# Seven f64 weight chunks loaded during the attention, the first gather moved to ScalarE's queue, and the ranking of the experts put ahead of all narrowing

## Chip, cores and metric

The kernel runs on one core of one Trainium2 chip. The metric is the device time of one execution in microseconds (us). A core has a matrix engine (TensorE, PE in the profile; PEld is its weight load), VectorE (DVE), ScalarE (ACT), GpSimd (POOL) and SyncE (SP, which here only issues transfers), 16 transfer engines, an on-chip memory of 128 partitions and the psum banks into which TensorE writes. ScalarE and GpSimd have transfer queues of their own as well.

## What is computed

Three stages follow one another; the host does no arithmetic.

```
scores = where(mask, q @ k.T / 8, -1e9)       # q, k, v: 2 x 8 heads x 576 x 64; half the heads
x = softmax(scores) @ v                       # see 32 keys back, half every 32nd key
x = x.transpose to (1152 tokens, 512)
logits = x @ w_gate; expert = argmax          # 8 experts, at most 288 tokens each, in order
y = relu(x_e @ w1[e]) @ w2[e]                 # w1: 8 x 512 x 1024, w2: 8 x 1024 x 512, f32
x = softmax weight of the chosen expert * y
out = max(0.01 h, h) @ w_out, h = x @ w_in    # w_in: 512 x 2048, w_out: 2048 x 512, f64 (16 MB)
```

## The kernel before

**Attention** (some 0 to 85 us). Sixteen units of two heads and one half each go through the engines in an order written out by hand: LOOP has a line of letters for each of 14 iterations, TAIL (lines 40 to 45) the order of the rest. A letter stands for a step of one engine. L issues loads on SP's queue (lines 808 to 824): at iteration 8 the second batch's local q and k, at 10 its v rows. While units finish, route_idx (line 606) picks each token's expert and its place among that expert's tokens, in four groups of tokens; scatter (g0 to g11 in TAIL, line 671) writes 96 token rows each with an indirect transfer on GpSimd's queue into the DRAM buffer xs, sorted by expert. route_gate (line 314) computes the softmax weights of a group's tokens: one exponential on ScalarE and six short steps on VectorE. route_order (o in TAIL, line 257) then ranks the experts by their number of tokens: a matmul sums the counts, and 16 short steps on VectorE give the experts' order (`by[:, 0]`, line 274), the largest load (`most`, line 279) and the offsets (`by[:, 1]`, line 282).

**The branch.** Lines 968 and 977 load these numbers into registers: the order on SP and ScalarE, the offsets on VectorE, `most` on every engine. GpSimd clears the four yT buffers (line 976), which lie where the attention's buffers were. Line 981 is a branch that every engine takes part in: its body, not run here, treats experts with too many tokens. It uses the same psum banks and transfer counters as the code behind it, so each engine passes an event there.

**Experts** (100 to 246 us). start() (line 896) issues on SP's queue the gather of the first expert's rows from xs (x_rows, line 840), two pairs of weights (load_pair, line 112: 512 KB of w1 on line 119, as much of w2 on line 121), the second expert's gather and two pairs more. A block of four matmuls of the identity (line 913) is issued ahead of the first transposes (x_cols, lines 846 to 850), which turn the gathered rows. Each expert then has eight steps of layer 1 (line 856, relu on ScalarE, line 857) and eight of layer 2 (line 863), two steps behind; VectorE adds an expert's four banks into yT (line 872) and so frees them. Pairs have four buffers (NA). Each step of layer 1 ends with pump(1, NX), one step of narrowing.

**Narrowing.** VectorE and ScalarE turn the f64 weights of the last stage into two f32 halves each, high and low. There are 16 chunks of 1 MB, loaded as two parts (load_wide, line 132; the tag wide has NW = 4 buffers, so four parts come in the attention, at iteration 10). A part takes three bit steps on VectorE (top, line 152; sign, 157; low, 162; the last also loads the part NW further on), a cast on ScalarE (high, 167) and a subtraction on VectorE (rest, 171). Six steps make a chunk; pump(n, used) runs the next n while fewer than `used` chunks are done, and NX = 10 chunks are to be narrowed before the last stage, into the tag hlx of a pool that takes the attention's space. start() runs the remaining route_gate and pump(6, NX) ahead of the branch's successors.

Within a `manual_schedule` block each engine keeps the written order. Where the steps of one block fall among those of another is left to a scheduler: it drew the gate and the first narrowing of start() ahead of the branch, in turns with route_order.

**Last stage** (246 to 455 us). Three blocks of 384 tokens, TensorE bound; narrowing of the other six chunks goes on beside the first block.

Of the kernel before, what the change touches and what calls it, by code (L numbers as in the profile page):

```python
# [8 lines left out]
F32 = mybir.dt.float32  # L9
F32R = mybir.dt.float32r  # L10
# [29 lines left out]

TAIL = """
sw ay0 pw ay1 cv my Rk Lk ev r1 dv xv az0 az1 Rk fy cw ew Lv Lk Rj dw cy Rj mz0 xw Lv Rv ey Rv Rl Lw Rl mz1 fz0
fz1 sy Lw i2 dy i2 cz0 xy i2 Rw i2 i2 cz1 sz0 ez0 i2 ez1 Ly i2 dz0 i2 Rw dz1 xz Ly i2 sz1 Ly i2 g5 Ry Lz Lz Lz
i3 i2 i2 i3 g6 i3 Rz Ry i3 Rz g7 wz1 i3 i3 Wy wz0 i3 i3 g8 i3 i3 g9 i3 i3 o g10 g11
# [5 lines left out]
def kernel(ctx, tc, q, k, v, w_gate, w1, w2, w_in, w_out, out, cap):  # L50
# [26 lines left out]
    wts = ctx.enter_context(tc.tile_pool(name="wts", bufs=1))  # L77
    dram = ctx.enter_context(tc.tile_pool(name="dram", bufs=1, space=bass.MemoryType.DRAM))
# [19 lines left out]
    NA, NX = 4, 10  # L98
# [24 lines left out]

    def hl_tile(i):
        a, b = chunks[i].shape[1:]
        tag, nb = ("hlx", NX) if i < NX else ("hl", NA) if i < NX + NA else ("hly", len(chunks) - NX - NA)
        hls[i] = pools[tag].tile([128, 2, a, b], F32R, tag=tag, name=tag, bufs=nb)
# [14 lines left out]
    def narrow(j):  # L142
        i, h = j // 2, j % 2
        a, b = chunks[i].shape[1:]
        hs = slice(h * a // 2, (h + 1) * a // 2)
        got = {}

        def top():
            if h == 0:
                hl_tile(i)  # L150
            tmp = got["tmp"] = wts.tile([128, a // 2, b], U32, tag="tmp", name="tmp", bufs=3)
            nc.vector.tensor_scalar(out=tmp, in0=wides[j][:, :, :, 1], scalar1=3, scalar2=0x3FFFFFFF,
                                    op0=ALU.logical_shift_left, op1=ALU.bitwise_and)

        def sign():
            tmp = got["tmp"]
            nc.vector.scalar_tensor_tensor(out=tmp, in0=wides[j][:, :, :, 1], scalar=0xC0000000, in1=tmp,
                                           op0=ALU.bitwise_and, op1=ALU.bitwise_or)

        def low():  # L160
            tmp = got["tmp"]
            nc.vector.scalar_tensor_tensor(out=tmp, in0=wides.pop(j)[:, :, :, 0], scalar=29, in1=tmp,
                                           op0=ALU.logical_shift_right, op1=ALU.bitwise_or)
            load_wide(j + NW)

        def high():
            nc.scalar.copy(out=hls[i][:, 0, hs], in_=got["tmp"].bitcast(F32))  # L167

        def rest():
            hl = hls[i]  # L170
            nc.vector.tensor_tensor(out=hl[:, 1, hs], in0=got["tmp"].bitcast(F32), in1=hl[:, 0, hs].bitcast(F32),  # L171
                                    op=ALU.subtract)

        return [top, sign, lambda: (low(), high()), rest]

    narrows = []
    spent = [0]

    def pump(n, used):
        for _ in range(n):  # L180
            if spent[0] < len(narrows) and spent[0] // 6 < used:
                narrows[spent[0]]()
                spent[0] += 1
# [143 lines left out]
    last = {}  # L327
# [5 lines left out]
    with ExitStack() as actx:  # L333
# [271 lines left out]
        def route_idx(r):  # L605
# [7 lines left out]
            if r == 2:  # L613
                t = wts.tile([TT, 2, 2 * G, E], F32, tag="tmp", name="gates", bufs=3)
                last["dl"], last["kp"] = t[:, 0], t[:, 1]
            own = slice((r - 2) * G, (r - 1) * G)
            dl = last["dl"][:, own] if r > 1 else att.tile([TT, G, E], F32, tag="dl", name="dl", bufs=2)
# [24 lines left out]
            kp = last["kp"][:, own] if r > 1 else att.tile([TT, G, E], F32, tag="kp", name="kp", bufs=2)  # L642
# [39 lines left out]
        with tc.manual_schedule():  # L682
# [62 lines left out]
            for it in range(NU - 2):  # L745
                us = todo.get(it, [])
                cur, prev = units[it], units[it - 1] if it else None
                for op in LOOP[it].split():
# [18 lines left out]
                    elif op == "L":  # L767
# [13 lines left out]
                        if it == 10:  # L781
                            load_vl(1)
                            for j in range(NW):
                                load_wide(j)
# [16 lines left out]
            for op in TAIL.split():  # L801
                if op in gens:
                    run(gens[op], 1)
                elif op == "o":
                    route_order(bank_t(), att)
                elif op[0] == "g":
# [81 lines left out]
    with ExitStack() as ectx:  # L888
# [7 lines left out]
        def start():  # L896
            xrs[0] = x_rows(wts, 0, 0, 2, WR[0] // 2, nc.sync)
            load_pair()
            load_pair()
            xrs[1] = x_rows(wts, 1, 0, 2, WR[1] // 2, nc.sync)  # L900
            for _ in range(NA - 2):
                load_pair()
            late = []
            for j in range(2 * len(chunks)):
                p = narrow(j)
                narrows.extend([p[0], lambda s=p[1], f=late: (s(), [x() for x in f]), p[2]])
                late = p[3:]
            narrows.append(late[0])
            route_gate(last["dl"], last["kp"], slice(TB, 2 * TB), ep)
            pump(6, NX)  # L910
            warm = bank("S")
            for i in range(2):
                nc.tensor.matmul(warm.rearrange("p (a b) -> p a b", a=4), ident,
                                 ident.unsqueeze(1).to_broadcast([128, 4, 128]), start=(i == 0), stop=(i == 1))
            xe_new(0)
            for c in range(KD):
                x_cols(xrs[0], xes[0], c, 2, WR[0] // 2, "L")

# [12 lines left out]
        def step(lay, e, m):  # L931
            p = (e * NF + m) // 2
            if lay == 1:
# [7 lines left out]
                pump(1, NX)  # L941
# [24 lines left out]
        with tc.manual_schedule():  # L966
# [10 lines left out]
            over = nc.values_load(most, min_val=0, max_val=3 * NT)  # L977

# [47 lines left out]
    with ExitStack() as mctx:  # L1026
# [6 lines left out]
        for i in range(len(items) + LAG):  # L1033
            if i < len(items):
# [5 lines left out]
                while spent[0] < min(len(narrows), 6 * (m // 2 * 2 + 2) + 2) and ch == 0:  # L1040
                    pump(1, 999)
# [67 lines left out]
```

## Time and profile before

| | us |
|---|---|
| median of 3 runs | 462.95 |
| runs | 462.08 to 463.44 |
| profiled execution, its own time | 461.31 |
| its span in the trace | 459.6 |
| TensorE busy | 428.0 (93%) |
| VectorE busy | 209.2 (46%) |
| ScalarE busy | 159.0 (35%) |
| GpSimd busy | 71.4 (16%) |

The times are those of whole executions, the span is what the trace covers of one of them. A busy share is an average over stages with different limits, so stretches are read one by one. The clock that TensorE was granted has two levels, 1.0 (2.4 GHz) and 0.5 (1.2 GHz); the mean of a stretch can lie between. A wait names the engine, the line and what came last before the wait ended. An event or a branch of an engine's sequencer has a q behind the engine's name (DVEq).

### The profile page before, as it was taken

How to read it: one execution, taken by the hardware profiler on the slowest of the kernel's cores; microseconds unless marked ns; L12 is line 12 of the kernel's file. 1: busy time of each engine (PE TensorE's matmuls, PEld its weight loads, DVE VectorE, ACT ScalarE, POOL GpSimd, SP SyncE). 2: the span in 40 equal slices, each digit the busy share in tenths (PEclk: the TensorE clock that was granted, in tenths of full speed). 3: DMA queues.
4: the chain of work that ended last, by engine and by line, in shares of the span. 5: the costliest groups of instructions: out<-in, count | busy, mean ns of one | idle time of the engine just before them, and what ended most of it. 6: DMA issues, size and time to landing. Idle time of an engine off the chain costs nothing.

```text
span 459.6 us, 7850 instructions
## 1 busy us (share of the span) xinstructions
PE 428.0 (93%) x2980; PEld 398.6 (87%) x2980; DVE 209.2 (46%) x472; ACT 159.0 (35%) x379; POOL 71.4 (16%) x127
## 2 busy tenths in 40 slices
PE   5999999159999999988999999999999999999994
PEld 5899999039999999987899898899899989998993
DVE  4677878851253351542302687783222233222220
ACT  4768776112222222222122433442422233322222
POOL 6252542730000001560000000000200000200002
PEclk9999999659999999999999999999999999999998
DMA  7999640369999899999992044200100000100001
GB/s 170 194 323 177 187 154 19 106 196 319 352 330 313 299 302 310 332 249 306 352 352 66 8 133 135 91 3 0 71 0 1 0 0 1 68 1 0 1 0 69
DMA packets 56566, 68.84 MB, mean 150 GB/s; under 512 B 20137, under 2 KB 36521, under 8 KB 56521
## 3 DMA queue, kind: packets, MB, share of 16 engines
q1 hardware_dynamic: 53691, 61.74, 45.0%
q0 software_dynamic: 1872, 4.73, 3.0%
q10 hardware_dynamic: 958, 1.80, 1.4%
q8 instruction: 25, 0.41, 0.4%
q14 instruction: 20, 0.16, 0.1%
HBM read 60.38 MB, written 7.87 MB: 149 GB/s over the span
## 4 chain that ended last, share of the span: by engine, by line
issue 44%; PE 24%; DMA 6%; POOL 2%; POOLq 0%; ACT 0%; SPq 0%; ACTq 0%
PE psS L856 12%; PE psL L863 11%; DMA xr<-xs 2%; DMA pair<-in_moe_w_dram 2%; POOL out_dram L1078 2%; DMA tb<-tab 1%; PE psT L849 1%; PE psL L849 0%; POOLq L1105 0%; ACT ht L857 0%; POOL gap L663 0%; SPq L121 0%; SPq L119 0%; ACT xe L850 0%; POOLq L1078 0%
## 5 line engine op out<-in xcount | busy, mean ns | idle before, releaser
L856 PE MATMUL psS<-xe,pair 128*128 128x128 f32 (+6 forms) x512 | 79.6, 300 | 1.9 <-DMA pair<-in_moe_w_dram 1.9
L863 PE MATMUL psL<-ht,pair 128*128 128x128 f32 (+6 forms) x512 | 79.8, 300 | 0.0
L856 PEld LDWEIGHTS psS<-xe,pair 128*128 128x128 f32 x512 | 73.0, 193 | 2.4 <-issue 2.3
L863 PEld LDWEIGHTS psL<-ht,pair 128*128 128x128 f32 x512 | 70.7, 190 | 0.5
L1053 DVE TENSOR_TENSOR r<-psS,r 128x384 f32<-128x384 f32 x48 | 26.7, 557 | 82.6 <-ACT r L1052 82.6
L857 ACT ACTIVATE ht<-psS 128x128 f32<-128x128 f32 (+6 forms) x64 | 19.2, 300 | 109.4 <-PE psS L856 101.6
L1052 ACT ACTIVATE r<-psS 128x384 f32<-128x384 f32 x48 | 23.6, 492 | 86.8 <-PE psS L1050 86.7
L1078 POOL DMA_INDIRECT out_dram<-o,tb x9 | 8.7, 962 | 239.9 <-ACT o L1077 239.1
L1047 PE MATMUL psS<-yc,hlx 128*128 128x384 f32 x120 | 40.6, 338 | 0.9 <-ACT yc L884 0.9
L1048 PE MATMUL psS<-yc,hlx 128*128 128x384 f32 x120 | 40.7, 339 | 0.0
L1056 DVE TENSOR_TENSOR g<-r,g 128x384 fp32r<-128x384 f32 x48 | 26.8, 559 | 27.8 <-ACT g L1055 27.8
L1055 ACT CAST g<-r 128x384 fp32r<-128x384 f32 x48 | 24.6, 513 | 31.7 <-DVE r L1053 31.7
L171 DVE TENSOR_TENSOR hlx<-tmp,hlx 128x512 fp32r<-128x512 f32 x20 | 13.8, 689 | 42.5 <-ACT hlx L167 42.5
L872 DVE TENSOR_TENSOR yT<-psL,yT 128x128 f32 (+6 forms) x32 | 9.2, 320 | 50.4 <-PE psL L863 50.3
L1070 PE MATMUL psL<-hlx,g 128*128 128x512 f32 x70 | 27.7, 396 | 0.0
L1069 PE MATMUL psL<-hlx,g 128*128 128x512 f32 x70 | 27.7, 395 | 0.0
L1068 PE MATMUL psL<-hlx,g 128*128 128x512 f32 x70 | 27.2, 389 | 0.0
L1050 PE MATMUL psS<-yc,hlx 128*128 128x384 f32 x120 | 25.6, 334 | 0.0
L456 PE MATMUL psS<-kT,qz 128*72 128x72 f32 (+1 forms) x224 | 25.1, 256 | 0.0
L1047 PEld LDWEIGHTS psS<-yc,hlx 128*128 128x128 f32 x120 | 22.5, 188 | 2.8 <-ACT yc L884 1.6
L456 PEld LDWEIGHTS psS<-kT,qz 128*72 128x72 f32 (+1 forms) x224 | 24.2, 162 | 0.0
L1048 PEld LDWEIGHTS psS<-yc,hlx 128*128 128x128 f32 x120 | 22.5, 188 | 1.2
(286 smaller groups left out, 757.7 us busy)
## 6 DMA issues: line engine op xcount, KB each, us to landing
pair<-in_moe_w_dram SPq DMA_DIRECT2D x64, 512.0 KB
wide<-in_moe_w_in_dram SPq DMA_DIRECT2D x16, 512.0 KB
wide<-in_moe_w_out_dram SPq DMA_DIRECT2D x16, 512.0 KB
xs<-zt SPq DMA_DIRECT2D x8, 384.0 KB
vl<-in_v_dram SPq DMA_DIRECT2D x12, 128.0 KB
qs<-in_q_dram SPq DMA_DIRECT2D x4, 288.0 KB
qs<-in_k_dram SPq DMA_DIRECT2D x4, 288.0 KB
vs<-in_v_dram SPq DMA_DIRECT2D x4, 288.0 KB
```

The lines of the kernel that those rows point to most:

```text
L456: nc.tensor.matmul(sv[:, n], lq, lk, start=False, stop=(n == nt - 1))
L856: nc.tensor.matmul(pt[:, :Wx], w[:, c, fs], xe[:, c, :Wx], start=(c == 0), stop=(c == KD - 1))
L863: nc.tensor.matmul(acc[n][:, :Wx], w[:, m % 2, n * 128:(n + 1) * 128], ht[:, :Wx], start=(m == 0), stop=(m == NF - 1))
L1047: nc.tensor.matmul(pt[:, :CS], wi[:, 0, c, fs], yc[c][:, 0], start=(c == 0), stop=False)
L1048: nc.tensor.matmul(pt[:, :CS], wi[:, 1, c, fs], yc[c][:, 0], start=False, stop=False)
L1050: nc.tensor.matmul(pt[:, :CS], wi[:, 0, c, fs], yc[c][:, 1], start=False, stop=(c == KD - 1))
L1053: nc.vector.tensor_tensor(out=r, in0=pt[:, :CS], in1=r, op=ALU.max)
L1055: nc.scalar.copy(out=g[:, 0], in_=r)
L1056: nc.vector.tensor_tensor(out=g[:, 1], in0=r, in1=g[:, 0].bitcast(F32), op=ALU.subtract)
L1068: nc.tensor.matmul(accs[ch][s], g[:, 0, ss], wo[:, 0, k % 2], start=(k == 0), stop=False)
L1069: nc.tensor.matmul(accs[ch][s], g[:, 0, ss], wo[:, 1, k % 2], start=False, stop=False)
L1070: nc.tensor.matmul(accs[ch][s], g[:, 1, ss], wo[:, 0, k % 2], start=False, stop=(k == NG - 1))
```

## The change

A pool `early` holds five buffers of 8 KB a partition. At iterations 9 to 13 of the attention SP loads one whole chunk each (load_whole); at iteration 13 it also loads four parts, those of chunks 5 and 6, where before the four parts of chunks 0 and 1 came at iteration 10. The narrowed values of chunks 0 to 4 go into the space of their own chunk, so that ScalarE's casts wait for both parts' low steps; the tag hlx has five buffers fewer. Narrowing steps are sorted anew. TAIL ends with G (the remaining route_gate) and N (six narrowing steps: the three bit steps of both parts of chunk 0), in the attention's block and behind route_order. The first gather is issued on ScalarE's queue ahead of the branch. start() no longer has the gate and pump(6, NX), but pump(4, NX) behind the first transposes. Each layer 1 step of the first two experts pumps two steps instead of one.

```diff
-i3 i2 i2 i3 g6 i3 Rz Ry i3 Rz g7 wz1 i3 i3 Wy wz0 i3 i3 g8 i3 i3 g9 i3 i3 o g10 g11
+i3 i2 i2 i3 g6 i3 Rz Ry i3 Rz g7 wz1 i3 i3 Wy wz0 i3 i3 g8 i3 i3 g9 i3 i3 o g10 g11 G N
...
+    early = ctx.enter_context(tc.tile_pool(name="early", bufs=1))
...
-    NA, NX = 4, 10
+    NA, NX, NE = 4, 10, 5
...
+    def load_whole(i):
+        a, b = chunks[i].shape[1:]
+        w = early.tile([128, a, b, 2], U32, tag=f"early{i}", name="whole", bufs=1)
+        nc.sync.dma_start(out=w.rearrange("p a b t -> p a (b t)"), in_=chunks[i].bitcast(U32))
+        wides[2 * i], wides[2 * i + 1] = w[:, :a // 2], w[:, a // 2:]
+
     def hl_tile(i):
         a, b = chunks[i].shape[1:]
-        tag, nb = ("hlx", NX) if i < NX else ("hl", NA) if i < NX + NA else ("hly", len(chunks) - NX - NA)
+        if i < NE:
+            hls[i] = early.tile([128, 2, a, b], F32R, tag=f"early{i}", name="hle", bufs=1)
+            return
+        tag, nb = ("hlx", NX - NE) if i < NX else ("hl", NA) if i < NX + NA else ("hly", len(chunks) - NX - NA)
...
-            load_wide(j + NW)
+            if j >= 2 * NE:
+                load_wide(j + NW)
 
         def high():
+            if h == 0:
+                hl_tile(i)
...
-        return [top, sign, lambda: (low(), high()), rest]
+        return [top, sign, low, high, rest]
+    AHEAD = 2
+    steps_of = [narrow(j) for j in range(2 * len(chunks))]
     narrows = []
+    late = [lambda: None, lambda: None]
+    for c in range(len(chunks)):
+        p, o = steps_of[2 * c], steps_of[2 * c + 1]
+        if c < NE:
+            narrows += [p[0], lambda p=p, f=late: (p[1](), f[0]()), p[2],
+                        o[0], lambda o=o, f=late: (o[1](), f[1]()), lambda p=p, o=o: (o[2](), p[3](), o[3]())]
+            late = [p[4], o[4]]
+            if c == 0:
+                narrows[5] = o[2]
+                late = [lambda p=p, o=o: (p[3](), o[3](), p[4]()), o[4]]
+        else:
+            if c == NE:
+                late = [lambda f=late: (f[0](), f[1]())]
+            narrows += [p[0], lambda p=p, f=late: (p[1](), f[-1]()), lambda p=p: (p[2](), p[3]())]
+            narrows += [o[0], lambda o=o, p=p: (o[1](), p[4]()), lambda o=o: (o[2](), o[3]())]
+            late = [o[4]]
+    narrows += late
...
                             load_vl(1)
-                            for j in range(NW):
+                        if it > 8:
+                            load_whole(it - 9)
+                        if it == NU - 3:
+                            for j in range(2 * NE, 2 * NE + NW):
                                 load_wide(j)
...
+                elif op == "G":
+                    route_gate(late_gates["dl"], late_gates["kp"], slice(TB, 2 * TB), att)
+                elif op == "N":
+                    for _ in range(6):
+                        narrows.pop(0)()
...
         def start():
-            xrs[0] = x_rows(wts, 0, 0, 2, WR[0] // 2, nc.sync)
             load_pair()
             load_pair()
...
-            late = []
-            for j in range(2 * len(chunks)):
-                p = narrow(j)
-                narrows.extend([p[0], lambda s=p[1], f=late: (s(), [x() for x in f]), p[2]])
-                late = p[3:]
-            narrows.append(late[0])
-            route_gate(last["dl"], last["kp"], slice(TB, 2 * TB), ep)
-            pump(6, NX)
...
                 x_cols(xrs[0], xes[0], c, 2, WR[0] // 2, "L")
+            spent[0] += 3 * AHEAD
+            pump(4, NX)
...
-                pump(1, NX)
+                pump(2 if e < 2 else 1, NX)
...
             over = nc.values_load(most, min_val=0, max_val=3 * NT)
+            xrs[0] = x_rows(wts, 0, 0, 2, WR[0] // 2, nc.scalar)
```

## Rows read from the trace of the kernel before

**Rows 1.** Windows: stretch, its us, busy us by engine, clock, DMA share, GB/s.
```profile
60.00:80.00 20.00, 19.97 (x231) 18.73 (x227) 16.40 (x57) 13.42 (x34) 6.24 (x9) 1.00 0.16 53
...
100.00:105.00 5.00, 4.30 (x20) 4.21 (x20) 2.72 (x9) 1.39 (x5) 0.00 (x0) 0.55 1.02 329
...
140.00:160.00 20.00, 20.00 (x144) 19.99 (x143) 8.11 (x16) 4.44 (x15) 0.00 (x0) 1.00 0.95 316
...
200.00:220.00 20.00, 17.15 (x132) 15.92 (x131) 7.37 (x15) 4.65 (x15) 4.42 (x8) 1.00 1.03 316
```

**Rows 2.** Timeline of TensorE from 84 to 104 us: start, us, line, operation.
```profile
84.80 0.24 PE L258 MATMUL psT<-ohs,ones 96*96 96x8 bf16 x1 [1.02 <-DVE ohs L656]
96.31 3.78 PE L913 MATMUL psS<-ident 128*128 128x512 f32 x4 [11.27 <-ACTq L981]
100.80 1.54 PE L849 MATMUL psL<-ident,xr 96*128 96x96 f32 x8 [0.70 <-DVEq L981]
102.13 2.18 PE L856 MATMUL psS<-xe,pair 128*128 128x192 f32 x6
```

**Rows 3.** Waits from 100 to 246 us: total, times, longest.
```profile
PE psS L856 <- DMA pair<-in_moe_w_dram: 1.9, 2, 1.4
...
PE psT L849 <- DMA xr<-xs: 1.5, 1, 1.5
```

**Rows 4.** Timeline of SP: the first two transfers of the experts.
```profile
95.00 0.36 SPq L843 DMA_DIRECT2D xr<-xs  x1
95.59 0.45 SPq L119 DMA_DIRECT2D pair<-in_moe_w_dram  x1
```

**Rows 5.** Line 981: events by queue, durations in ns, first and last start.
```profile
L981 SPq EVENT_SEMAPHORE  x8: 17/17/17, 92.8 to 93.3; - x8
...
L981 ACTq COMPARE_BRANCH  x1: 50/50/50, 93.6 to 93.6; - x1
...
L981 DVEq COMPARE_BRANCH  x1: 72/72/72, 95.8 to 95.8; - x1
L981 ACTq EVENT_SEMAPHORE  x1: 17/17/17, 96.2 to 96.2; - x1
L981 DVEq EVENT_SEMAPHORE  x1: 21/21/21, 100.7 to 100.7; - x1
...
  PEld psL L849: 2.3, 1
```

**Rows 6.** Timeline of VectorE from 84 to 96 us.
```profile
84.12 0.18 DVE L321 RECIPROCAL ps__3605<-ps__3605 96x6 f32<-96x6 f32 x1
...
84.81 0.41 DVE L152 TENSOR_SCALAR tmp<-wide 128x512 uint32<-128x512 uint32 x1
...
85.26 0.69 DVE L157 SCALAR_TENSOR_TENSOR tmp<-wide,tmp 128x512 uint32<-128x512 uint32 x1
...
86.01 0.68 DVE L162 SCALAR_TENSOR_TENSOR tmp<-wide,tmp 128x512 uint32<-128x512 uint32 x1
...
87.81 0.23 DVE L270 TENSOR_TENSOR pick<-more,index 1x64 f32<-1x64 f32 x1
...
90.10 0.21 DVE L272 TENSOR_REDUCE by<-pick 1x8 int32<-1x64 f32 x1
...
92.32 2.15 DVE L152 TENSOR_SCALAR tmp<-wide 128x512 uint32<-128x512 uint32 x1
```

**Rows 7.** Timeline of GpSimd: the last scatter, and the clearing of yT.
```profile
87.79 0.92 POOL L672 DMA_INDIRECT xs<-xra,slot  x1 [0.22 <-issue]
90.41 5.29 POOL L976 MEMSET yT<- 128x1440 f32 x4 [1.71 <-issue]
```

**Rows 8.** Windows of half a us: the one behind the last scatter.
```profile
90.00:90.50 0.50, 0.00 (x0) 0.00 (x0) 0.27 (x2) 0.04 (x1) 0.09 (x1) 0.50 0.01 0
```

**Rows 9.** Timeline of ScalarE: a cast.
```profile
90.46 0.62 ACT L167 CAST hlx<-tmp 128x512 fp32r<-128x512 f32 x1 [8.45 <-DVE by L272]
```

**Rows 10.** Chain of waits, pieces in order of time: start, us, what.
```profile
111.48 1.30 PE psS L856 x8
```

More of the change, by code (lines that the diff above doesn't have):

```diff
@@ L148, in top @@
         def top():
-            if h == 0:
-                hl_tile(i)
             tmp = got["tmp"] = wts.tile([128, a // 2, b], U32, tag="tmp", name="tmp", bufs=3)
@@ L180, in pump @@
         for _ in range(n):
-            if spent[0] < len(narrows) and spent[0] // 6 < used:
-                narrows[spent[0]]()
+            if narrows and spent[0] // 6 < used:
+                narrows.pop(0)()
                 spent[0] += 1
@@ L325, in route_gate @@
         nc.vector.tensor_tensor(out=tabsb[:, T, 1], in0=ps_, in1=ks_, op=ALU.mult)
-    last = {}
+    late_gates = {}
     def run(gen, n=99):
@@ L614, in route_idx @@
                 t = wts.tile([TT, 2, 2 * G, E], F32, tag="tmp", name="gates", bufs=3)
-                last["dl"], last["kp"] = t[:, 0], t[:, 1]
+                late_gates["dl"], late_gates["kp"] = t[:, 0], t[:, 1]
             own = slice((r - 2) * G, (r - 1) * G)
-            dl = last["dl"][:, own] if r > 1 else att.tile([TT, G, E], F32, tag="dl", name="dl", bufs=2)
+            dl = late_gates["dl"][:, own] if r > 1 else att.tile([TT, G, E], F32, tag="dl", name="dl", bufs=2)
             nc.vector.tensor_tensor(out=dl, in0=lg, in1=lmx.unsqueeze(2).to_broadcast([TT, G, E]), op=ALU.subtract)
@@ L641, in route_idx @@
             yield
-            kp = last["kp"][:, own] if r > 1 else att.tile([TT, G, E], F32, tag="kp", name="kp", bufs=2)
+            kp = late_gates["kp"][:, own] if r > 1 else att.tile([TT, G, E], F32, tag="kp", name="kp", bufs=2)
             nc.vector.scalar_tensor_tensor(out=kp, in0=rk[:, 0], scalar=float(cap), in1=oh[:, T],
@@ L805 @@
                     route_order(bank_t(), att)
+                elif op == "G":
+                    route_gate(late_gates["dl"], late_gates["kp"], slice(TB, 2 * TB), att)
+                elif op == "N":
+                    for _ in range(6):
+                        narrows.pop(0)()
                 elif op[0] == "g":
@@ L1039 @@
                     run(p, 1)
-                while spent[0] < min(len(narrows), 6 * (m // 2 * 2 + 2) + 2) and ch == 0:
+                while narrows and spent[0] < 6 * (m // 2 * 2 + 2) + 2 and ch == 0:
                     pump(1, 999)
```

## Prediction

> **What bounds it now.** I read the stage windows first: TensorE is busy throughout 60 to 80 and 140 to 160 us, and 17.15 of 20 us late in the experts [rows 1]. What an edit can give back is therefore a TensorE gap, and there are two kinds. The timeline of TensorE shows the large one: between the matmul that sums the experts' counts (84.80) and the first transposes of gathered rows (100.80) there is only a block of four warm-up matmuls at 96.31; the first expert's layer starts at 102.13 [rows 2]. The granted clock of 100 to 105 us is 0.55 in the mean, so it was at its half level (1.2 of 2.4 GHz) until 104.5 [rows 1]: from 100.80 on, 3.7 us of work went at half speed. The waits of 100 to 246 us show the small gaps: 1.5 us for a gather and 1.9 us for a pair of expert weights, 3.4 us together [rows 3]. The transfer engines have little room there, with a share of 0.95 and 1.03, but only 0.16 in 60 to 80 us [rows 1].
>
> What ends the large gap is read from the view of the branch's line, 981. The transposes write the psL banks, and their weight load is put down to VectorE's event there, at 100.7, not to the gather, asked for at 95.0 [rows 4]. VectorE reached the branch at 95.8 and needed 4.9 us to come out of it; ScalarE reached it at 93.6 and needed 2.6 [rows 5]. So VectorE's passage is the last wait, and what VectorE does ahead of the branch sets it: gate, ranking and narrowing in turns, then more narrowing [rows 6].
>
> **Ranking ahead.** Between 84.81 and 87.81 VectorE does four steps of ranking and five of narrowing; the rest of the ranking, 12 steps, runs undisturbed from 87.81 to 90.31, 0.21 us each [rows 6]. Four steps would take 0.85 us, so about 1.75 us goes; the gate's steps, now behind, gave way in the dispatch chain ahead of it for an estimated 0.25 more. Ranking ends at 88.3 instead of 90.3, and the experts' order is known at 86.3.
>
> **Gate and first narrowing (G, N).** They stand behind the ranking and still ahead of the branch. The gate is six steps of 0.18, 1.1 us. N is two times 0.41, 0.69 and 0.68, 3.6 us [rows 6]. Before, VectorE spent 90.3 to 95.8 on later narrowing, among it a wait for ScalarE's cast (which now comes behind the branch) and one L152 of 2.15 instead of 0.41 us. That step ran while GpSimd cleared yT, 5.29 us from 90.41 [rows 6, 7]. Clearing needs the attention's space, which the gate now holds until 89.4, so it runs from 89.4 to 94.7, beside N. The first L152 should be in before it; the second comes at 91.2 and can lose 0 to 3.5 us, and I take 1.4, near the 1.7 that the row shows. Here a page of the Trainium skill speaks against the change: "SBUF — State Buffer", section "Who interferes with whom", has VectorE's two-port forms and GpSimd exclude each other for a whole instruction, the loser blocked outright. The slow L152 agrees; by the rule at its worst both would wait and the passage would not move, as in the second rival.
>
> Sum: 88.3 + 1.1 + 3.6 + 1.4 = 94.4; the register loads, which before began under the last steps, bring the branch to about 95.0, 0.8 earlier (93.6 without a block; 98 with 3.5 and another chunk's steps drawn ahead). The passage takes 2.6 us (ScalarE's) to 4.9 (VectorE's own, with weight loads running since 95.6 [rows 4]). I take 3.7, midway, as the loads start about when VectorE arrives: out at 98.7, **2.1 us** earlier than the 100.80. Ends: 96.2 and 102.9.
>
> **The first gather on ScalarE's queue.** The last scatter is issued at 87.79 [rows 7] and no data moves from 90.0 on [rows 8]; ScalarE knows the order at 87, waits for the scatter and can ask at some 90.7, against 95.0. Queued behind that wait on ScalarE is only its own passage, 91.3 + 2.6 = 93.9 (96.2 before), which the warm-up block follows. Landing took at most 5.7 us (95.0 to 100.7) and at least its data's 1.3 (0.38 MB at some 300 GB/s); with a free queue I take the middle, 3.3: 94.0. There is a new wait: SP passes eight events at line 981 [rows 5], which I read as one for each counter of the transfers asked for so far; the gather will be among them, so SP is held until 94.0. Behind it stand four pairs (eight loads) and the second gather; the first load goes out at 94.2 to 95.6, against 95.59. The first weights needed at most 6.5 us (95.59 to 102.13), 1.3 of it shared with the gather, so 5.2 now: landed at about 100, just in time for a layer that starts 1.3 us behind transposes at 98.7. They are what is late next. The clock rose 3.7 us after the transposes began; I keep that lag, at no gain.
>
> **Seven chunks early.** Five whole chunks (5.2 MB) join 2.1 MB of halves. SP has nothing to ask for after the attention's last v rows until the experts, and 60 to 80 us moved 53 GB/s [rows 1]: at some 300 GB/s six of the seven MB take 20 us from about 52. Beside them run the first scatters, whose buffers are wanted 10 us later; TensorE was full at a share of 0.95 too [rows 1], so I cost it at 0 (to 1 us). The experts' phase loses 5.2 MB of the some 45 that it carries (145 us at 316 GB/s), and the rest of the halves is asked for before expert 4. The late gather and pair then meet weight loads alone: **3.3 us** of the 3.4 go (bounds 0 and 3.4).
>
> **Doubled pumps in experts 0 and 1.** Each slot now has two narrowing steps. A chunk costs VectorE 2 x (0.41 + 0.69 + 0.68 + 0.69) = 4.9 us, the last figure an estimate from L157, and ScalarE two casts of 0.62 [rows 6, 9]; both are spread over three slots, each a layer step and an output step of 1.30, so 7.8 us [rows 10]. VectorE is filled to 63%, the cover stays. An expert's psL banks are freed by VectorE behind up to 2 us of narrowing: I add 0.3 us for both boundaries (0 to 2). Using the whole chunk's space in place makes both casts wait for both low steps; they stand behind the slot's relu, at nothing while VectorE is ahead.
>
> **Sum:** -2.1 - 3.3 + 0.3 = -5.1 us. The profiled execution took 461.31 (459.6 of span and 1.7 around it), 1.6 less than the median of 462.95; taken from that, **457.8**.
>
> **Rivals.** (1) *The clock is back sooner.* If VectorE is out at 97.6 or before, the transposes follow the warm-up block (93.9 to 97.7) without a gap, and the half-speed stretch lies under it: 3.2 + 1.85 + 3.3 = 8.3, 454.6. For it: the warm-up block with a gap behind it did not raise the clock, the unbroken work from 100.80 did [rows 1, 2]. Against: it needs a passage near 2.6 us. 0.12. (2) *The start doesn't move.* N, the gate and the blocked L152 keep VectorE until 95.8 or later, or the gather is in fact placed behind the branch; only the small gaps go: 459.6. For it: as many narrowing steps still precede the branch. 0.20. (3) *The small gaps stay*, because transfers slow down for other reasons (a share of 1.03 moved no more than one of 0.95, 316 GB/s [rows 1]): 460.8. 0.10. (4) *Neither:* 462.9. 0.08. (5) *Slower: the doubled pump holds ScalarE.* Its casts wait for VectorE's low step, the next relu queues behind them, and TensorE waits for its psS bank. In a chunk's third slot that is 0.69 + 0.69 + 0.68 on VectorE and 1.24 of casts, less the 1.3 of an output step: 2.0 us, and 10 for five chunks: 467.8. It decides once VectorE lags by more than a slot's 2.6 us. Against: 63%. 0.08. My own case has 0.42.
>
> **Numbers.** 0.3%, 1.4 us, is about what a measurement can tell from no change. Faster takes most of my case and of rivals 1 to 3: 0.78; same 0.13; slower 0.09. The range leaves out part of rival 1 below, and 4 and 5 above: 454.2 to 462.0.
>
> **What would show it.** Ranking without narrowing in it, 2 us earlier; ScalarE asking for the first gather near 90.7; SP's first pair only once that has landed; an L152 of over 1 us beside the clearing of yT; VectorE's event at line 981 near 98.7 and transposes right behind; no TensorE wait for a gather or pair after 190 us; transfers near 300 GB/s until 72 us. The prediction is wrong if VectorE's event stays at 100 or later, if the transposes or the first layer wait for something else (gather, weights), or if TensorE stalls in the first two experts.

## Result and the profile after

The changed kernel took **456.55 us** in the median of four executions (456.20 to 456.88), the kernel before on the same chip 462.85 (462.08 to 463.44): a ratio of 0.9865, 95% interval 0.9836 to 0.9893. That is faster by 6.3 us and inside the range; the forecast was 457.8. The ratios here and below are worked out from fast executions alone and can lie up to 0.3% from the quotient of the medians beside them.

| | before | after |
|---|---|---|
| profiled execution, own time | 461.31 | 456.36 |
| its span | 459.6 | 454.6 |
| ranking ends on VectorE | 90.31 | 88.46 |
| first transposes | 100.80 | 100.08 |
| first expert layer | 102.13 | 101.41 |
| matmul of equal number near 199 us | 198.99 | 198.20 |
| matmul of equal number near 235 us | 235.09 | 230.12 |

The table already says where the time went. Of the 5.0 us between the two traces, **0.7 came at the start and 4.2 between 199 and 235 us**. Nothing else moved: from 101 to 199 us, and again from 235 us to the end, the distance stays the same to 0.1 us. (The medians lie 6.3 us apart; the profiled execution of the kernel before was faster than its four others. The remaining 1.3 us can't be looked for in these two traces.)

Windows of the changed kernel, in the stretches of [rows 1]:

```profile
60.00:80.00 20.00, 19.97 (x229) 18.74 (x226) 16.38 (x58) 13.44 (x34) 6.43 (x9) 1.00 0.65 253
100.00:105.00 5.00, 4.92 (x24) 4.92 (x25) 2.44 (x5) 2.52 (x7) 0.00 (x0) 0.64 1.03 311
140.00:160.00 20.00, 20.00 (x144) 19.99 (x143) 9.12 (x19) 5.01 (x16) 0.00 (x0) 1.00 1.02 342
200.00:220.00 20.00, 20.00 (x161) 19.15 (x161) 1.77 (x7) 3.30 (x13) 3.29 (x7) 1.00 1.02 263
```

At 60 to 80 us the transfers moved 253 GB/s in place of 53, and TensorE lost nothing by it. At 200 to 220 us TensorE works all 20 us (17.15 before), and VectorE, which was busy for 7.37 us there, mostly with narrowing, has 1.77. The transfer share is as full as before.

The start, in the timeline of TensorE [rows 2] and in the view of the branch, now line 1017 [rows 5]:

```profile
84.77 0.24 PE L292 MATMUL psT<-ohs,ones 96*96 96x8 bf16 x1 [0.97 <-DVE ohs L690]
95.20 3.78 PE L946 MATMUL psS<-ident 128*128 128x512 f32 x4 [10.19 <-ACTq L1017]
100.08 1.54 PE L891 MATMUL psL<-ident,xr 96*128 96x96 f32 x8 [1.10 <-DVEq L1017]
101.41 2.76 PE L898 MATMUL psS<-xe,pair 128*128 128x192 f32 x9
```

```profile
L1017 SPq EVENT_SEMAPHORE  x8: 17/17/17, 91.2 to 95.0; - x8
...
L1017 ACTq COMPARE_BRANCH  x1: 50/50/50, 90.4 to 90.4; - x1
...
L1017 ACTq EVENT_SEMAPHORE  x1: 17/17/17, 95.1 to 95.1; - x1
L1017 DVEq COMPARE_BRANCH  x1: 72/72/72, 95.8 to 95.8; - x1
L1017 DVEq EVENT_SEMAPHORE  x1: 21/21/21, 100.0 to 100.0; - x1
```

VectorE reaches its branch at 95.8, exactly as before, though the ranking ended 1.9 us sooner. What ate that is in its timeline (to be held against [rows 6]) and in GpSimd's [rows 7]:

```profile
88.25 0.21 DVE L306 TENSOR_REDUCE by<-pick 1x8 int32<-1x64 f32 x1
...
89.18 0.42 DVE L162 TENSOR_SCALAR tmp<-whole 128x512 uint32<-128x512 uint32 x1
...
90.97 2.90 DVE L162 TENSOR_SCALAR tmp<-whole 128x512 uint32<-128x512 uint32 x2
93.79 1.27 DVE L167 SCALAR_TENSOR_TENSOR tmp<-whole,tmp 128x512 uint32<-128x512 uint32 x2
94.99 0.68 DVE L172 SCALAR_TENSOR_TENSOR tmp<-whole,tmp 128x512 uint32<-128x512 uint32 x1
```

```profile
89.46 5.64 POOL L1011 MEMSET yT<- 128x1440 f32 x4 [1.37 <-issue]
```

The first L162 is in before GpSimd clears yT and takes 0.42 us. The other two run beside the clearing and take 2.90 together, 1.38 and 1.59 in the single records. N has two of these steps; the third, and a second L167 near 94.4, belong to the next chunk and were drawn ahead of the branch.

### The profile page after: what moved, and what is told of

Its sections match the earlier page's. It is cut to its first block, busy times and chain, and to the rows that moved or that the text cites. A ratio compares the mean times of both kernels' runs of the same rounds, so it can differ in the third digit from the quotient of the medians.

```text
span 454.6 us, 7859 instructions
## 1 busy us (share of the span) xinstructions
PE 426.9 (94%) x2980; PEld 398.1 (88%) x2980; DVE 209.8 (46%) x472; ACT 158.5 (35%) x379; POOL 69.4 (15%) x127
## 4 chain that ended last, share of the span: by engine, by line
issue 44%; PE 29%; POOL 2%; DMA 1%; POOLq 0%; SPq 0%
PE psS L898 14%; PE psL L905 14%; POOL out_dram L1114 2%; DMA tb<-tab 1%; PE psT L891 1%; PE psL L891 0%; POOLq L1141 0%; POOL gap L697 0%; SPq L123 0%; SPq L121 0%; POOLq L1114 0%; SPq L1060 0%
## 5 line engine op out<-in xcount | busy, mean ns | idle before, releaser
L899 ACT ACTIVATE ht<-psS 128x128 f32<-128x128 f32 (+6 forms) x64 | 19.1, 301 | 102.1 <-PE psS L898 93.3
L1083 PE MATMUL psS<-yc,hle 128*128 128x384 f32 x72 | 24.5, 340 | 1.0 <-ACT yc L926 1.0
L1084 PE MATMUL psS<-yc,hle 128*128 128x384 f32 x72 | 24.4, 339 | 0.0
L500 DVE TENSOR_REDUCE mx<-psS 72x8 f32<-72x576 f32 (+2 forms) x17 | 13.5, 795 | 8.1 <-PE psS L490 8.1
L1106 PE MATMUL psL<-hlx,g 128*128 128x512 f32 x42 | 16.6, 396 | 0.0
L1105 PE MATMUL psL<-hlx,g 128*128 128x512 f32 x42 | 16.6, 395 | 0.0
L1104 PE MATMUL psL<-hlx,g 128*128 128x512 f32 x42 | 16.3, 389 | 0.0
L1084 PE MATMUL psS<-yc,hlx 128*128 128x384 f32 x48 | 16.3, 340 | 0.0
L1084 PE MATMUL psS<-yc,hl 128*128 128x384 f32 x48 | 16.3, 340 | 0.0
L1083 PE MATMUL psS<-yc,hlx 128*128 128x384 f32 x48 | 16.1, 336 | 0.0
```

What stands on the lines that cost most here:

```text
L899: nc.scalar.activation(out=ht[:, :Wx], in_=pt[:, :Wx], func=ACTF.Relu)
L1083: nc.tensor.matmul(pt[:, :CS], wi[:, 0, c, fs], yc[c][:, 0], start=(c == 0), stop=False)
L1084: nc.tensor.matmul(pt[:, :CS], wi[:, 1, c, fs], yc[c][:, 0], start=False, stop=False)
L1105: nc.tensor.matmul(accs[ch][s], g[:, 0, ss], wo[:, 1, k % 2], start=False, stop=False)
```

## Experiments

Two things had to be explained: why the start moved so little, and which part of the change removed the late waits. Twelve kernels ran, on three chips, each beside the kernel before. There single executions of one kernel lie up to 8.6 us apart, so medians tell apart only what differs by 2 to 3 us; for less, the traces are read. First the yardstick, **the changed kernel again**, without an edit:

> The changed kernel once more, beside its own variants on one chip, as their yardstick. All theories expect the ratio of the first comparison, 0.984 to 0.989 of the kernel before, a first transpose near 100.1 us, and no idle time of TensorE over 0.3 us between the first transposes and 247 us. If instead the gaps among the later experts come back here, they depend on the chip and not only on the program, and what the variants show by them weighs less.

Measured: 458.82 against 464.34, ratio 0.987 (0.981 to 0.993). The gain stands, and no wait over 0.3 us follows the transposes until 247 us. The start does not stand as still: VectorE reached its branch at 97.3 and left at 102.7, so the transposes began at 102.76. With one step a slot (below), where the code up to the first layer is the same, they began at 99.78; in the kernel before at 100.80, and at 103.19 in its variant with the same start. So the 0.7 us that the first two traces show at the start is less than what single executions of the same code differ by, and is not shown to be a gain.

### Which part removes the late waits

**One narrowing step a slot**, everything else as changed:

```
-                pump(2 if e < 2 else 1, NX)
+                pump(1, NX)
```

> One narrowing step a slot in all experts; the same loads in all, but the last ten f64 parts are asked for in experts 2 to 6 and not by expert 4. Theory E: what counts is that no f64 loads run beside the later experts; then TensorE waits for a gather or a pair again, 1 to 3.4 us in all: 457.5 to 460. Rival F: the smaller amount (5.2 MB instead of 10.5) is enough by itself, at any pace: 456 to 457, no wait.

Measured: 464.17, ratio 0.9977 (0.9947 to 1.0007). The whole gain is gone. **The f64 chunks late** as well:

```
-                pump(2 if e < 2 else 1, NX)
+                pump(1, NX)
+                k = e * NF + m
+                if k in (1, 7):
+                    load_whole(3 + k // 7)
+                if k in (13, 19):
+                    load_wide(2 * NE + k // 19 * 2)
+                    load_wide(2 * NE + k // 19 * 2 + 1)
```

(and these loads, with that of the third chunk, taken out of the attention)

> Five of the seven f64 chunks are asked for among the first three experts again and not in the attention, and one narrowing step a slot is made; everything of the start is as in the changed kernel. Theory A (what the change gained in the experts is that the late experts have neither f64 loads nor narrowing beside them): the time of the run with one step a slot or worse, 0.995 to 1.005 of the kernel before, with TensorE waits of 0.4 to 3 us for pair weights or rows. Theory B (the doubled pumps alone did it, the place of the loads is nothing): exactly the run with one step a slot, 0.998, and the same three waits. Theory C (neither; the gain is in the start): 0.986 to 0.990.

Measured: 462.72, ratio 0.9964 (0.9925 to 1.0004), not to be told from the run before it (its profiled execution, 464.92, was the slowest of its twelve). And the opposite, **the kernel before with nothing but the doubled steps**:

```
-                pump(1, NX)
+                pump(2 if e < 2 else 1, NX)
```

> The kernel before with two narrowing steps a slot in the first two experts, its f64 chunks still asked for half by half as narrowing goes on. Theory A (the gain in the experts comes from traffic: seven chunks of f64 no longer share the queues with weights and rows there, and the doubled steps only move what is left to the front): the same bytes meet the weights earlier, TensorE waits for pairs or rows somewhere between 110 and 180 us in place of 204 to 222, and the time is 0.997 to 1.010 of the kernel before. Theory B (the doubled steps alone did it): the three waits at 204, 212 and 222 go and nothing replaces them, 0.990 to 0.993. The start is that of the kernel before under both.

Measured: 464.66, ratio 1.0015 (0.998 to 1.005). By the time this is no gain, as theory A said; by the waits of its trace theory B holds. Waits from 101 to 246 us, of one step a slot, of the late chunks, and of the kernel before with two steps:

```profile
PE psS L898 <- DMA pair<-in_moe_w_dram: 3.8, 2, 3.1
...
PE psT L891 <- DMA xr<-xs: 0.5, 1, 0.5
```

```profile
PE psS L895 <- DMA pair<-in_moe_w_dram: 2.8, 1, 2.8
...
PE psT L888 <- DMA xr<-xs: 0.4, 1, 0.4
```

```profile
PE psT L849 <- DMA xr<-xs: 0.5, 1, 0.5
```

With one step a slot the waits of [rows 3] are back, wherever the chunks are loaded; with two steps they are gone even from the kernel before (its 0.5 us is at 172 us). What the two steps change is when the last f64 halves are asked for. Transfers issued from 185 to 247 us, in the kernel before, with one step a slot, and in the kernel before with two:

```profile
wide<-in_moe_w_out_dram SPq DMA_DIRECT2D x4, 512.0 KB
wide<-in_moe_w_in_dram SPq DMA_DIRECT2D x3, 512.0 KB
```

```profile
wide<-in_moe_w_out_dram SPq DMA_DIRECT2D x4, 512.0 KB
wide<-in_moe_w_in_dram SPq DMA_DIRECT2D x2, 512.0 KB
```

```profile
wide<-in_moe_w_out_dram SPq DMA_DIRECT2D x2, 512.0 KB
```

The changed kernel issues none there. So seven, six and six halves go with late waits of 3.3, 3.8 and 2.8 us, and two or none with no wait after 185 us. The same holds for the changed kernel run again and for four variants below (ranking last, narrowing behind, clearing behind, none ahead): no half after 185 us, no wait there. Two do not fit. The profiled execution of the run with the gather on SyncE waits 2.2 us near 207 us with no half asked for after 185 (at 464.88 it was the slowest of its eight), and the last run below waits 1.06 and 0.87 us at 201 to 205 with none asked for between 138 and 236. So late halves go with late waits, but such waits can come without them.

Why did the kernel before gain no time from two steps? In its trace TensorE makes up 3.0 us on the kernel before between 114 us and the end, but the start came later by more than 2 us, though the edit changes nothing there. Its narrowing step beside the clearing took longer still (compare 2.15 in [rows 6]), and VectorE left the branch at 103.1:

```profile
92.42 3.38 DVE L152 TENSOR_SCALAR tmp<-wide 128x512 uint32<-128x512 uint32 x1
```

```profile
L981 DVEq COMPARE_BRANCH  x1: 72/72/72, 97.2 to 97.2; - x1
L981 DVEq EVENT_SEMAPHORE  x1: 21/21/21, 103.1 to 103.1; - x1
```

Whether all its executions started so late is not known; one trace cannot tell, and this one, 460.85, is of the second fastest of twelve. So by the time neither part alone gives a gain, not the early chunks with the new start (0.9977) and not the doubled steps (1.0015); both together do. What the traces add, that the late waits go with the early asking, explains the first; why the second is no faster stays open.

### The start

**The first gather on SyncE again, behind its branch:**

```
-            xrs[0] = x_rows(wts, 0, 0, 2, WR[0] // 2, nc.scalar)
...
         def start():
+            xrs[0] = x_rows(wts, 0, 0, 2, WR[0] // 2, nc.sync)
             load_pair()
```

> Theory A: VectorE's passage of the branch ends the large gap, so the place of the first gather is worth next to nothing. With the gather back on SP's queue behind the branch, VectorE still reaches line 981's branch at about 95.9 and comes out at 100 to 100.8; transposes there; total 456.3 to 457.3, no gap of TensorE late in the experts. Rival B: the gather's early start is what the start gained; then the transposes wait for its landing, past 101, and the total is 457.5 to 459.

Measured: 459.8, ratio 0.9907 (0.9872 to 0.9942). **The ranking behind gate and narrowing:**

```
-... i3 i3 o g10 g11 G N
+... i3 i3 G N o g10 g11
```

> The gate and the first narrowing put ahead of the ranking, the reverse of the change. Theory A: VectorE has the same work ahead of the branch, so it gets there at 94 to 96 as before, and the total stays within 1 us, 455.7 to 457.5, though the order of the experts is known 4.7 us later. Rival C: early ranking is what counts, because registers, gather and weights start from it: the first weights then land past 102, and the total is 458 or more.

Measured: 458.77, ratio 0.9908 (0.9873 to 0.9942). Against the changed kernel's 458.82 (on another chip, where the kernel before took 464.34 in place of 464.42) that is 1.0 and 0.0 us, and 1.7 us each by the ratios, less than these runs resolve: taking back either the queue of the gather or the place of the ranking shows no loss. The branch views of the two say why. ScalarE and VectorE, first with the gather on SyncE, then with the ranking last:

```profile
L1017 ACTq COMPARE_BRANCH  x1: 50/50/50, 87.9 to 87.9; - x1
...
L1017 ACTq EVENT_SEMAPHORE  x1: 17/17/17, 91.0 to 91.0; - x1
...
L1017 DVEq COMPARE_BRANCH  x1: 72/72/72, 95.7 to 95.7; - x1
L1017 DVEq EVENT_SEMAPHORE  x1: 21/21/21, 102.2 to 102.2; - x1
```

```profile
L1017 ACTq COMPARE_BRANCH  x1: 50/50/50, 93.4 to 93.4; - x1
...
L1017 DVEq COMPARE_BRANCH  x1: 72/72/72, 94.5 to 94.5; - x1
...
L1017 ACTq EVENT_SEMAPHORE  x1: 17/17/17, 97.7 to 97.7; - x1
L1017 DVEq EVENT_SEMAPHORE  x1: 21/21/21, 97.9 to 97.9; - x1
```

VectorE's passage is no constant: 6.5 us in the first, 3.5 in the second, where the later ranking holds SyncE's loads back too, to 98.57, behind that passage. With the ranking last, the narrowing also stands ahead of GpSimd's clearing, and the two L162 that are slow in the changed kernel take 0.76 us together:

```profile
87.22 0.76 DVE L162 TENSOR_SCALAR tmp<-whole 128x512 uint32<-128x512 uint32 x2
```

**Narrowing behind the transposes**, held there by a copy that reads their result:

```
-... o g10 g11 G N
+... o g10 g11 G
...
+            hold = const.tile([1, 1], F32, name="hold")
+            nc.vector.tensor_copy(out=hold, in_=xes[0][0:1, KD - 1, 0:1])
+            for _ in range(6):
+                narrows.pop(0)()
             spent[0] += 3 * AHEAD
```

> The first narrowing (N) behind the first transposes, held there by a copy of one gathered value. Theory A: VectorE reaches the branch at about 90.5 and is out by 95; the transposes then follow the warm-up block at about 99.0 and the first weights (landed at 99.6) are next: 1.1 us earlier, and up to 1.8 more where the clock comes back sooner; total 453.7 to 455.6. Rival D: the gap is set by weights or gather as well, the transposes stay at 100 or later: 456.2 to 457.

Measured: 460.25, ratio 0.9918 (0.9885 to 0.9951). The start did what was hoped, and TensorE then stopped:

```profile
L1021 DVEq COMPARE_BRANCH  x1: 72/72/72, 90.8 to 90.8; - x1
...
L1021 DVEq EVENT_SEMAPHORE  x1: 21/21/21, 91.4 to 91.4; - x1
```

```profile
95.94 3.78 PE L946 MATMUL psS<-ident 128*128 128x512 f32 x4 [10.55 <-ACTq L1021]
99.51 1.34 PE L891 MATMUL psL<-ident,xr 96*128 96x96 f32 x8
100.68 2.79 PE L898 MATMUL psS<-xe,pair 128*128 128x192 f32 x16
106.51 2.12 PE L898 MATMUL psS<-xe,pair 128*128 128x192 f32 x8 [3.04 <-ACT ht L899]
```

The passage took 0.6 us and the transposes follow the warm-up block without a gap. But on ScalarE the casts of the narrowing now stood ahead of the first Relu, which came at 106.14, and waited for VectorE's steps:

```profile
105.09 1.14 ACT L180 CAST hle<-tmp 128x512 fp32r<-128x512 f32 x2 [3.84 <-DVE tmp L172]
106.14 0.32 ACT L899 ACTIVATE ht<-psS 128x192 f32<-128x192 f32 x1
```

**The clearing of yT behind the transposes:**

```
-            for t in yT:
-                nc.gpsimd.memset(t, 0.0)
...
+            nc.gpsimd.tensor_copy(out=gap, in_=xes[0][0:1, KD - 1, 0:1])
+            for t in yT:
+                nc.gpsimd.memset(t, 0.0)
             spent[0] += 3 * AHEAD
```

> GpSimd clears the four sums behind the first transposes and not beside VectorE's narrowing; all else as changed. Theory A (the early ranking was eaten because VectorE's narrowing ran beside the clearing: two 0.42 us steps took 1.38 and 1.59): these take 0.42 each, VectorE is at its branch near 93.7 in place of 95.8, through it by 98, and the transposes follow the warm-up at 99.0: 1.0 us less than the changed kernel, ratio about 0.984. Theory B (VectorE's passage ends when the weight loads let its code through, whenever it begins): the branch is reached earlier but left near 100 as before, and the time stays within 0.4 us of the changed kernel's.

Measured: 460.23, ratio 0.9921 (0.9886 to 0.9955). It is no clean test of the clearing, since most of N was also placed behind the branch; VectorE passed from 90.8 to 91.4. TensorE started at 98.67 and stopped too, for weights; the clearing met narrowing in its new place:

```profile
98.67 0.82 PE L891 MATMUL psL<-ident,xr 96*128 96x96 f32 x8
99.53 2.87 PE L898 MATMUL psS<-xe,pair 128*128 128x192 f32 x16
105.42 2.85 PE L898 MATMUL psS<-xe,pair 128*128 128x192 f32 x8 [3.02 <-DMA pair<-in_moe_w_dram]
```

```profile
101.91 3.77 DVE L162 TENSOR_SCALAR tmp<-whole 128x512 uint32<-128x512 uint32 x1
```

So a start that is 1.4 us earlier ran into the second pair of weights, asked for only once SyncE was through its branch. **No narrowing ahead, and the first pair ahead of the branch:** N and the four pumped steps go, a hold as above stays, a pair is asked for behind the gather and ahead of the branch, and

```
+            load_pair()
...
-                pump(2 if e < 2 else 1, NX)
+                pump(3 if e < 2 else 1, NX)
```

> No narrowing ahead of the branch at all, three steps a slot in the first two experts in place of it, and SyncE asks for the first pair of weights ahead of its branch. Theory A (narrowing ahead of the branch is what keeps VectorE from passing it early; the run with the narrowing behind the transposes lost its gain only because ScalarE's casts stood ahead of the first Relu, a 3.0 us wait of TensorE): VectorE is at its branch near 91, the transposes follow the warm-up at once, near 99.0 to 99.5, no wait over 0.5 us follows, and the time is 1 us under the changed kernel, ratio 0.983 to 0.986. Theory B (the passage of ScalarE is held by whatever is moved at that time): with the first pair's megabyte in the queues it leaves its branch at 97 or later in place of 95.1, the warm-up begins that much later, and the time is 1 to 2 us over the changed kernel.

Measured: 457.83, ratio 0.9871 (0.981 to 0.9931). VectorE went through from 90.7 to 91.3, the transposes began at 99.33, and the matmul that runs at 116.11 in the changed kernel ran at 113.86. By 177 us that lead of 2.2 us was gone, in waits at 144, 150 and 168 us: theory A's start came, its time did not.

### How far an early start carries

**Two steps over four experts** in place of three over two (`pump(2 if e < 4 else 1, NX)`):

> As the run with no narrowing ahead of the branch and the first pair ahead of it, but two steps a slot over four experts in place of three over two. Theory A (its lead of 2.2 us at 114 us was given back at 144, 150 and 168 us because three steps a slot ask for the remaining f64 halves too early, beside the weights): those waits go, and the trace ends 1.5 to 2.2 us ahead of the changed kernel's 454.6. Theory B (weights themselves arrive no sooner, since the queues are full from 140 us on whatever the steps do): waits of about 2 us in all remain somewhere between 140 and 230 us, and the span is 454.2 to 455.2.

Measured: 459.78, ratio 0.9931 (0.9896 to 0.9966). Waits of 1.3 us at 167, 1.6 at 183 and 0.4 at 207 us, more than theory B's 2. **Gathers and four pairs ahead of the branch**, all on SyncE:

```
+            xrs[0] = x_rows(wts, 0, 0, 2, WR[0] // 2, nc.sync)
+            load_pair()
+            load_pair()
+            xrs[1] = x_rows(wts, 1, 0, 2, WR[1] // 2, nc.sync)
+            for _ in range(NA - 2):
+                load_pair()
```

> As the run with two steps a slot over four experts, and on SyncE, ahead of its branch: the first gather, four pairs of weights and the second gather. Theory A (SyncE's own passage, 91.3 to 97.5 us in the run with one pair ahead, leaves the queues half empty, 0.55 of their time at 96 to 104 us, and ScalarE without a gather passes by 91): the warm-up ends at 96 to 97, transposes follow by 97, TensorE never waits over 0.5 us for a pair before 140 us, the lead over the changed kernel is 3 us at 114 us, and the queues being ahead by three megabytes hold it: span 451 to 452.5. Theory B (the queues are the bound from 140 us on): as much lead at 114 us, but given back to under 1.5 us by 230 us: span 453.2 to 455. Theory C (four megabytes delay the first gather or its rows): transposes later than 100, span over 456.

Measured: 457.18, ratio 0.987 (0.9829 to 0.9911). The first layer started at 96.87, 4.5 us before the changed kernel's, and the lead was still 4.5 at 161 us. Its span is 454.3, so all but 0.3 went again, as in theory B: 1.87 us at 164 for rows, 1.53 at 181 for a pair, and some at what follows each stop. The rows had been asked for at 153.2; on SyncE the second half of a pair waited for the same transfer's counter:

```profile
153.21 0.27 ACTq L885 DMA_DIRECT2D xr<-xs  x1
```

```profile
160.82 0.38 SPq L121 DMA_DIRECT2D pair<-in_moe_w_dram  x1
165.80 0.37 SPq L123 DMA_DIRECT2D pair<-in_moe_w_dram  x1
```

So the last run also moved the four halves that only the last stage needs **behind the last pair**:

```
-            if j >= 2 * NE:
+            if 2 * NX <= j + NW < 2 * NX + NW:
+                later.append(j + NW)
+            elif j >= 2 * NE:
                 load_wide(j + NW)
...
         if p >= NPAIR:
+            load_wide(later.pop(0))
             return
```

(with three steps a slot in two experts)

> As the run with gathers and four pairs ahead of SyncE's branch, but with three narrowing steps a slot in the first two experts, and the four f64 halves that only the last stage narrows (they were asked for at 150 to 171 us) are asked for behind the last pair of weights. Theory A (the lead of 4.5 us at 160 us was given back because these halves and the rows of an expert share full queues: a row gather asked for at 153.2 us landed at 165.8, and a pair's second half waited for it): no wait of TensorE over 0.6 us between 110 and 247 us, first matmul of the last stage at 244 us, span 450 to 451.5, ratio 0.975 to 0.98. Theory B (weights and rows alone fill the queues, the halves were not what was too much): waits of 2 to 4 us in all remain between 140 and 230 us, span 453 to 455. Theory C (the last stage now waits for its first halves or for narrowing): TensorE idle over 1 us near 250 to 262 us, the lead at 240 us kept and lost there.

Measured: 457.48 against 465.81 there, ratio 0.9805 (0.9765 to 0.9845), the lowest of all; the fastest execution took 454.51. Its interval still overlaps the changed kernel's 0.9836 to 0.9893, and its own median is no lower than that of the run before it (457.18, beside 463.64 for the kernel before), so that it beats the changed kernel is not shown. In its profiled execution, the slowest of its six, the lead was 2.3 us from 151 to 199 us and fell to 1.5 us behind at 211: rows asked for at 191.4 came for 202.1 (1.06 us of wait), a pair cost 0.87, and the clock then fell for 3.4 us. The waits over 0.25 us between 140 and 230 us come to 2.7 us in all, as theory B said; the fall of the clock, which made the span 456.1, stood in none of the three. Why queues whose share is 0.9 to 1.0 move only 198 GB/s at 180 to 200 us here (280 in the changed kernel), beside the scatters of the tables, stays open; leaving those scatters out was not tried.

## Why the prediction was right, point by point

- **The sum** gave 457.8 for 456.55, and its closeness is luck: its two main terms were wrong in opposite directions. -2.1 for the start was -0.7 between the two traces (and not shown to be a gain at all), -3.3 for the small gaps was -4.2, and the +0.3 for the doubled pumps was not seen. By its own sign of being wrong, VectorE's event at 100 or later, the part on the start failed: the event came at 100.0.
- **Ranking ahead:** as said. It ended at 88.46 for 88.3.
- **Gate and N to the branch at 95.0:** this step failed, by 0.8 us. One blocked L162 with a loss of 1.4 was in the sum. There were two, with losses of 0.96 and 1.17 us against 0.42, and a second chunk's L162 and L167 were drawn ahead (2.2 us), which stood only in the bound of 98; a shorter gate and shorter register loads gave some back. The Trainium skill, "SBUF — State Buffer", section "Who interferes with whom", has the loser of such a meeting blocked outright, and the trace agrees: 1.38, 1.59, 3.38 and 3.77 us beside the clearing in three kernels, 0.42 without it. In the single records each of these steps, and the 2.15 of [rows 6], ends 0.27 to 0.29 us behind the end of one of GpSimd's four clearing steps (1.29 to 1.58 us each), and a step that waits can let more than one of them pass: one, one, three, three, and two. So the loss comes in whole clearing steps.
- **The passage of 3.7:** it was 4.16, and the runs show 0.6 to 6.5. Midway between two rows was a fair size, but the premise, that a queue's passage has a size of its own, was not.
- **ScalarE's gather:** asked for at 89.94 (said: 90.7). ScalarE's passage was mis-sized: 4.7 us instead of 2.6, so the warm-up block came at 95.20, not 93.9. SyncE was held as said, to 95.04, and its first pair went out at 95.29.
- **Rival 2** (the start does not move) gave the right mechanism for the start, with N, gate and blocked steps filling VectorE until 95.8. Its 459.6 was too high by 3.0: the gaps gave 0.9 more, the start 0.7 in these traces, and the rest is what the medians lie further apart than the traces.
- **The small gaps:** the waits of [rows 3] went, as said. They hold 3.33 us of idle time, and the three stops cost 4.2: on average each stop costs 0.28 us more than TensorE's idle time. The credit was wrong as well. The step led with the 5.2 MB that leave the experts' phase; the runs show that their removal alone gives nothing (464.17 with one step a slot). In the traces the waits go where the last halves are asked for earlier; in time that alone gave nothing either (464.66 for the kernel before with two steps), only both together.
- **The doubled pumps**, entered at +0.3 as a cost, are what moves the halves, and without them the gain is gone. Rival 5, which saw them as the danger, did not come: no stop of TensorE over 0.3 us in the first two experts.
- **Seven chunks early at 0:** right; TensorE is as busy at 60 to 80 us as before.

## What to carry to other kernels

When a prefetch queue and a computation share the transfer engines, look at when the last item that is not urgent is asked for, not only at the bytes: with the end of the narrowing in front of a tight stretch the trace was 4 us shorter there, and a start 4.5 us earlier left 0.3 in its trace because the next limit stood 60 us on. Treat an engine's way out of a branch as a time of its own that ran from 0.6 to 6.5 us here, and look at what is moved while an engine on the path passes. If a step is moved ahead of a barrier, list what else the scheduler can draw ahead with it.

## What the runs showed that was not expected

- **VectorE's passage of a branch** took 0.6 us in the six traces where it was reached by 90.8 us, and 3.5, 4.1, 4.2, 4.9, 5.4, 5.9, 6.1 and 6.5 where it was reached from 94.5 on. The traces list loads of code among the transfers, as packets of 8 KB of the kind `instruction`. In each of the eight long passages one of them ends 1.5 to 1.7 us before VectorE's event; in the six short ones none falls between branch and event. The longest passage, with the gather on SyncE, has just one, which began 4.6 us behind the branch with the queues full (a share of 1.07; transfers of code from 95.7 to 102.1 us):

```profile
q14 instruction: 1, 0.01, 0.3%
```

With the ranking last, no weight load was asked for until that passage was over; the first such packet began 1.4 us behind the branch, and the passage still took 3.5. So a long passage goes with a load of code, and that it waits behind weights there fits these numbers. It was not tested by itself: the packets name no engine, and the six short passages are also those of the kernels that had most or all of N behind the branch.
- **The clock behind the warm-up block.** In [rows 2] and after, a gap follows the block and the half level holds until 3.7 and 3.6 us after the transposes began, in three more traces with a gap until 5.2 to 6.1 us after. In the other two (late chunks, and the kernel before with two steps) the clock came up at 97.5 and 100.9, fell again, and was back at 107.8 and 107.7. In the seven traces with no gap behind the block it was up 3.1 to 4.9 us after the block's own start. In the run with the clearing behind the transposes it was up 3.5 us after the block's start; but after the stop of 3.0 us it fell back to the half level for 3.4 us:

```profile
95.00:98.50 3.50, 3.39 (x4) 1.41 (x5) 0.00 (x0) 0.00 (x0) 0.00 (x0) 0.50 0.43 140
98.50:105.50 7.00, 3.94 (x26) 3.32 (x24) 4.81 (x3) 2.31 (x7) 5.13 (x5) 0.99 0.99 304
105.50:108.90 3.40, 3.40 (x11) 3.40 (x12) 3.33 (x8) 1.26 (x3) 0.00 (x0) 0.50 1.08 278
```

- The same followed the stop of 3.1 us at 202 us in the run with one step a slot, two stops of 1.06 and 0.87 us close together in the last run, and, there for 6.8 us, two of 1.50 and 0.65 us close together in the run with the gather on SyncE. The stops of 1.5 us and less in the kernel before, 6.5 us apart and more, and those of 1.87 and 1.53 us in the run with gathers and four pairs ahead, brought no fall. A long stop therefore costs about half of those 3.4 us on top of itself: the one of 3.1 us set TensorE back by 4.9 against the changed kernel.
- **A row gather of 304 KB took over 12 us** beside full queues (153.2 to 165.8), and held up a weight load on another engine's queue that was to use the same counter.
